# Linear attention with decay and two projections: another order of the instructions behind the opening

## The chip, the cores and the metric

The kernel runs on one core of a Trainium2 chip. The metric is the time of the program on the device in microseconds (us); it is taken as the median of several runs.

## The reference

q, k and v are 4 x 8 x 768 x 64 (batch, heads, positions, head width). Attention goes through blocks of 64 positions with a state of 64 x 64 for each batch and head, and what it gives is the input x (3072 tokens x 512) of two projections with a nonlinear step between them:

```python
for b in range(S // 64):
    intra = einsum('bhic,bhjc->bhij', qb, kb) * Dmask        # lam ** (i - j), i >= j
    intra = einsum('bhij,bhjd->bhid', intra, vb)
    inter = einsum('bhid,bhde->bhie', qb * lam_pow, kv_state)
    out[:, :, sl] = intra + inter
    kv_state = lam_block * kv_state + einsum('bhsd,bhse->bhde', kb * rev_pow, vb)
x = out.transpose(0, 2, 1, 3).reshape(3072, 512)
h = x @ w_in                                                  # 512 x 2048
g = h + sin(alpha * h) ** 2 / (alpha + 1e-9)
y = g @ w_out                                                 # 2048 x 512
```

## The kernel before

The attention is cut into 24 steps, t = 0 to 23, of 128 positions of one batch each. The projections go over 6 chunks, c = 0 to 5, of 512 tokens, four steps each. The program is first recorded as a list of operations, each with a name, an engine, what it reads and writes, and then ordered; the names are those of the lists below:

- "load k9.0e" and the like are transfers by SyncE (SP) of a part of q, k or v (lines 856 and 865); loads number n serves steps 2n and 2n + 1. The tiles k32, q32 and v32 are rings.
- ks, qs and vs with a step's number bring keys, queries and values to bf16 (line 1020 for keys and queries, with a factor; line 1044, a cast, for values). They run on VectorE (DVE), ScalarE (ACT) or GpSimd (POOL). qk2 and v2 are rings too.
- DT is a transposing transfer on SP that turns scaled keys and queries into the layout that TensorE (PE) wants (line 1054).
- S, Z, I and O are PE's scores (line 1096), state (1121, 1147) and outputs (1168) of a step; mask is DVE's product of the scores with the decay (1103, 1109), Zf, Zs the state's copies (1196, 1202, 1208), x the copy of the output to xT (1188).
- A c.m is the first product for one block of 128 of the 2048 columns: four matmuls into one PSUM bank (line 1234). sin c.m (ACT, line 1246), sq c.m (the square, ACT line 1255 or DVE and POOL line 1256) and g c.m follow. g (DVE, line 1260) adds the square, scaled, to the bank's h, and with that gives the bank back. For some columns of chunks 0 and 1 the tokens are taken in halves, h0 and h1.
- B c.s.m4 is a quarter of the second product for 128 tokens: four matmuls (line 1313). After the fourth, o copies the bank (line 1330) and st stores it. The last 128 tokens are done in three pieces of 256, 128 and 128 columns, B5.3.0 to B5.3.2 (lines 1281 to 1292).

There are six PSUM banks in M_ps for A, B and the attention's outputs. Which operation stands where on an engine is a written list, `ORDER`, with one list for each engine; the planner takes an engine's next operation from the head of its list only, and its cost table decides no more than which bank an operation gets. `ON` names the engine of an operation where it can run on several. `GATE` holds transfers back: the operation named on the left also waits for the one on the right.

```python
for a, b in TUNE["GATE"].items():
    named[a].deps.add(named[b])
```

Every engine works through its own list in order, and waits at an operation until what it depends on is done; so one that waits holds up all behind it on its engine.

Of the kernel before, what the change touches and what calls it, by code (L numbers as in the profile page):

```python
# [28 lines left out]
    GATE={'quad q1': 'E_i0',  # L29
          'quad v2': 'ks2',  # L30
          'quad k3': 'R_f',
          'quad k4': 'cT3.0',
          'quad q4': 'cT0.0',
          'quad v4': 'g0.1h0',
          'quad k5': 'g0.8',
# [3 lines left out]
          'quad q7': 'mask3',
          'quad v7': 'sq0.11',  # L40
          'load k4.0e': 'B0.3.3',
          'load v4.0': 'qs10',
          'load v4.0e': 'qs10',
          'load k5.0': 'B0.3.3',
          'load k5.0e': 'sin1.1h0',
          'load v5.0': 'sq1.8',
          'load q5.1': 'A1.0h0',
          'load v6.0': 'ks16',
          'load v6.0e': 'A2.9',
          'load k6.1e': 'g2.0',  # L50
          'load q6.1': 'S10',
          'load q7.0': 'Zs8',
          'load k7.1e': 'O11',
          'DT13': 'sin2.13',
          'load k8.0': 'o7',
          'load v8.0': 'sin2.11',
          'load k8.1': 'g2.4',
          'load k8.1e': 'A2.6',
          'DT15': 'Zs10',
# [1 line left out]
          'load v9.1': 'Z16f',
          'load k10.0': 'B2.2.1',
          'load k10.1': 'sin2.15',
          'load v10.1': 'qs21',
          'load v10.1e': 'A3.9',
          'DT18': 'ks19',
# [16 lines left out]
    ON={'sq2.11': 'DVE',  # L83
        'sq0.14': 'POOL',
        'sq3.0': 'DVE',
        'sq1.0h1': 'ACT',
        'sq2.4': 'ACT',
        'sq4.1': 'ACT',
# [1 line left out]
        'sq3.5': 'ACT',  # L90
        'sq3.14': 'ACT',
        'sq4.4': 'DVE',
        'sq5.14': 'ACT',
        'sq5.15': 'ACT',
        'qs1': 'POOL',
        'sq3.7': 'DVE',
        'sq3.15': 'DVE',
        'sq5.3': 'ACT',
        'vs8': 'POOL',
        'Zs8': 'POOL',  # L100
        'Zs10': 'POOL',
        'sq1.12': 'ACT',
        'sq2.0': 'ACT',
# [1 line left out]
        'sq2.14': 'ACT',
        'sq3.11': 'ACT',
        'sq4.6': 'DVE',
        'sq5.1': 'DVE',
        'qs0': 'POOL',
        'Z1f': 'ACT',  # L110
        'sq0.2h1': 'ACT',
        'sq0.4': 'ACT',
        'sq1.4h0': 'DVE',
        'qs15': 'DVE',
        'Zs14': 'DVE',
        'sq3.12': 'ACT',
        'sq3.13': 'ACT',
        'vs21': 'POOL',
        'cT0.1': 'ACT',
        'qs3': 'POOL',  # L120
        'cT3.0': 'ACT',
        'sq0.15': 'ACT',
        'vs4': 'DVE',
        'ks5': 'DVE',
        'Z6f': 'ACT',
        'qs7': 'POOL',
        'vs7': 'POOL',
# [1 line left out]
        'Z7f': 'ACT',
        'vs11': 'DVE',  # L130
        'Zs17': 'DVE',
        'sq3.8': 'ACT',
        'x19': 'DVE',
        'Zs21': 'DVE',
        'sq4.15': 'DVE',
        'ks1': 'POOL',
        'ks0': 'DVE',
        'Zs1': 'ACT',
        'Zs2': 'DVE',
        'Zs3': 'DVE',  # L140
        'sq0.0h0': 'POOL',
        'sq0.7': 'ACT',
        'sq0.9': 'DVE',
        'qs4': 'POOL',
        'qs5': 'POOL',
        'vs5': 'POOL',
        'cT6.1': 'ACT',
        'qs14': 'DVE',
        'x14': 'DVE',
        'sq3.4': 'DVE',  # L150
        'sq3.10': 'ACT',
        'ks20': 'DVE',
        'sq4.0': 'DVE',
        'ks21': 'DVE',
        'vs22': 'DVE',
        'sq4.8': 'ACT',
        'sq4.12': 'ACT',
        'sq5.4': 'ACT',
        'sq5.5': 'ACT',
        'o20': 'DVE',  # L160
        'o21': 'DVE',
        'Z2f': 'ACT',
        'Zi3': 'DVE',
        'sq0.0h1': 'DVE',
        'sq0.5': 'DVE',
        'sq0.8': 'POOL',
        'sq0.13': 'ACT',
        'cT4.1': 'ACT',
        'Zs4': 'POOL',
        'qs6': 'POOL',  # L170
        'Zs6': 'POOL',
        'o2': 'DVE',
        'ks8': 'DVE',
        'ks9': 'DVE',
        'vs9': 'DVE',
        'x8': 'DVE',
        'sq1.6': 'DVE',
        'sq1.7': 'DVE',
        'Zs9': 'DVE',
        'ks11': 'DVE',  # L180
        'sq1.10': 'POOL',
        'sq1.11': 'ACT',
        'qs12': 'DVE',
        'sq1.14': 'ACT',
        'sq1.15': 'POOL',
        'Zs11': 'DVE',
        'ks13': 'DVE',
        'sq2.10': 'ACT',
        'vs15': 'DVE',
        'sq2.12': 'ACT',  # L190
        'ks17': 'DVE',
        'sq3.1': 'ACT',
        'vs17': 'DVE',
        'o8': 'DVE',
        'sq3.3': 'ACT',
        'sq3.6': 'ACT',
        'ks19': 'DVE',
        'sq3.9': 'ACT',
        'qs19': 'DVE',
        'vs19': 'DVE',  # L200
        'o10': 'DVE',
        'qs21': 'DVE',
        'x20': 'DVE',
        'ks22': 'DVE',
        'ks23': 'DVE',
        'sq4.9': 'DVE',
        'qs23': 'DVE',
        'sq4.10': 'DVE',
        'o14': 'DVE',
        'sq4.11': 'DVE',  # L210
        'sq4.14': 'ACT',
        'x23': 'DVE',
        'sq5.2': 'DVE',
        'sq5.6': 'ACT',
        'sq5.7': 'POOL',
        'o18': 'DVE',
        'sq5.11': 'POOL',
        'sq5.13': 'ACT'},
# [1248 lines left out]
```

## Time and profile before

| | us |
|---|---|
| median of three runs | 214.68 (214.08 to 215.11) |
| profiled execution | 216.0 |
| its span | 214.1 |
| PE busy | 204.3 |
| DVE, ACT, POOL busy | 140.9, 127.0, 69.3 |

The profile is of one execution. Its span is what the trace covers; the time beside it is the device's. The granted clock of PE was 1.00 throughout. Rows of the timeline give the start, the time, the engine, the line, the operation and its tiles, and in brackets how long the engine had been idle before and what ended that.

### The profile page before, as it was taken

How to read it: one execution, taken by the hardware profiler on the slowest of the kernel's cores; microseconds unless marked ns; L12 is line 12 of the kernel's file. 1: busy time of each engine (PE TensorE's matmuls, PEld its weight loads, DVE VectorE, ACT ScalarE, POOL GpSimd, SP SyncE). 2: the span in 40 equal slices, each digit the busy share in tenths (PEclk: the TensorE clock that was granted, in tenths of full speed). 3: DMA queues.
4: the chain of work that ended last, by engine and by line, in shares of the span. 5: the costliest groups of instructions: out<-in, count | busy, mean ns of one | idle time of the engine just before them, and what ended most of it. 6: DMA issues, size and time to landing. Idle time of an engine off the chain costs nothing.

```text
span 214.1 us, 5329 instructions
## 1 busy us (share of the span) xinstructions
PE 204.3 (95%) x2216; PEld 112.8 (53%) x2216; DVE 140.9 (66%) x245; ACT 127.0 (59%) x233; POOL 69.3 (32%) x88
## 2 busy tenths in 40 slices
PE   7898999999799999999999998899999999999995
PEld 7657654657555455444455543344555444454454
DVE  2497795767789862685667866958879744355511
ACT  3662989936787337877445598624665716657411
POOL 4397129810176205654700130400411101116100
PEclk9999999999999999999999999999999999999999
DMA  6999999987998899777899889989521201050015
GB/s 178 276 256 212 216 219 275 230 184 185 200 163 179 177 191 233 142 216 164 177 161 236 179 174 186 157 196 154 123 52 49 90 11 49 2 194 3 0 63 182
DMA packets 86985, 33.90 MB, mean 158 GB/s; under 512 B 68786, under 2 KB 83506, under 8 KB 86962
## 3 DMA queue, kind: packets, MB, share of 16 engines
q1 hardware_dynamic: 79616, 22.88, 54.0%
q0 software_dynamic: 2688, 4.19, 11.1%
q10 hardware_dynamic: 4658, 6.50, 8.6%
q8 instruction: 17, 0.28, 0.5%
q14 instruction: 6, 0.05, 0.1%
HBM read 27.27 MB, written 6.29 MB: 157 GB/s over the span
## 4 chain that ended last, share of the span: by engine, by line
PE 64%; DMA 19%; DVE 6%; ACT 4%; POOL 3%; issue 2%; SPq 1%; ACTq 0%; DVEq 0%; POOLq 0%
PE M_ps L1313 30%; PE M_ps L1234 25%; DMA q<-in_q_dram 8%; DMA k<-in_k_dram 5%; DMA w<-in_moe_w_out_dram 4%; DVE gT L1260 3%; DMA alpha_sb<-in_moe_alpha_dram 3%; PE M_ps L1147 2%; POOL qk L1020 2%; PE M_ps L1281 2%; ACT t L1246 2%; PE A_ps L1096 2%; PE M_ps L1168 1%; DVE qkT L1071 1%; ACT u L1255 1%
## 5 line engine op out<-in xcount | busy, mean ns | idle before, releaser
L1234 PE MATMUL M_ps<-xT,w 128*128 128x512 bf16 (+1 forms) x424 | 88.6, 359 | 2.4 <-DVE gT L1260 2.3
L1260 DVE SCALAR_TENSOR_TENSOR gT<-u,r_sb,M_ps 128x512 bf16<-128x512 bf16 (+1 forms) x106 | 69.8, 692 | 30.1 <-POOL u L1256 15.3
L1313 PE MATMUL M_ps<-w,gT 128*128 128x512 bf16 x368 | 87.8, 380 | 1.2 <-DVE gT L1260 0.8
L1246 ACT ACTIVATE t<-M_ps,alpha_sb 128x512 bf16<-128x512 f32 (+1 forms) x106 | 65.2, 646 | 32.2 <-PE M_ps L1234 28.5
L1234 PEld LDWEIGHTS M_ps<-xT,w 128*128 128x128 bf16 x424 | 46.6, 114 | 39.0 <-DVE gT L1260 4.1
L1256 POOL TENSOR_TENSOR u<-t 128x512 bf16<-128x512 bf16 x27 | 27.9, 1041 | 86.0 <-ACT t L1246 81.9
L1313 PEld LDWEIGHTS M_ps<-w,gT 128*128 128x128 bf16 x368 | 34.1, 98 | 40.5 <-DVE gT L1260 1.8
L1255 ACT ACTIVATE u<-t 128x512 bf16<-128x512 bf16 x46 | 28.4, 628 | 0.9 <-ACT t L1246 0.2
L1020 POOL TENSOR_TENSOR qk<-q,L 128x512 bf16<-128x512 f32 x14 | 14.5, 1045 | 23.3 <-DVE qk L1020 14.8
L1188 ACT CAST xT<-M_ps 128x512 bf16<-128x512 f32 x14 | 8.1, 587 | 21.2 <-PE M_ps L1121 17.5
L1109 DVE TENSOR_TENSOR S_m<-A_ps,maskl 128x768 bf16<-128x768 f32 x16 | 15.2, 951 | 3.1 <-PE M_ps L1147 1.7
L1256 DVE TENSOR_TENSOR u<-t 128x512 bf16<-128x512 bf16 x23 | 10.1, 443 | 6.0 <-ACT t L1246 5.8
L1020 POOL TENSOR_TENSOR qk<-k,L 128x512 bf16<-128x512 f32 x9 | 9.4, 1045 | 10.6 <-DMA k<-in_k_dram 10.5
L1330 ACT COPY osb<-M_ps 128x512 f32<-128x512 f32 x13 | 7.6, 585 | 8.4 <-PE M_ps L1313 8.3
L826 PE MATMUL M_ps<-zeros 128*128 128x128 bf16 (+1 forms) x62 | 8.4, 317 | 1.2 <-DVE zeros L903 1.2
L1330 DVE COPY osb<-M_ps 128x512 f32<-128x512 f32 x7 | 4.7, 685 | 7.3 <-PE M_ps L1313 7.3
L1121 PE MATMUL M_ps<-v,qk 64*64 64x64 bf16 x320 | 8.3, 193 | 0.9 <-DVE S_m L1103 0.7
L1168 PE MATMUL M_ps<-S_m,v 64*64 64x128 bf16 (+1 forms) x384 | 9.0, 208 | 0.0
L1103 DVE TENSOR_TENSOR S_m<-A_ps,maskq 128x1024 bf16<-128x1024 f32 x6 | 7.3, 1218 | 2.1 <-PE A_ps L1096 2.1
L1020 DVE TENSOR_TENSOR qk<-k,L 128x512 bf16<-128x512 f32 x11 | 7.4, 683 | 1.8 <-DMA k<-in_k_dram 1.8
L1202 DVE TENSOR_TENSOR Zf<-M_ps,Zf 128x256 f32<-128x256 f32 x12 | 5.0, 420 | 5.4 <-ACT xT L1188 5.3
L1096 PE MATMUL A_ps<-qkT 64*64 64x128 bf16 (+1 forms) x352 | 8.2, 210 | 0.2 <-DVE qkT L1071 0.2
(72 smaller groups left out, 135.0 us busy)
## 6 DMA issues: line engine op xcount, KB each, us to landing
q<-in_q_dram SPq DMA_DIRECT2D x24, 256.0 KB, 5.4
out_dram<-osb ACTq DMA_DIRECT2D x23, 256.0 KB, 2.3
v<-in_v_dram SPq DMA_DIRECT2D x32, 128.0 KB, 4.3
k<-in_k_dram SPq DMA_DIRECT2D x32, 128.0 KB, 4.6
v<-in_v_dram SPq DMA_DIRECT2D x8, 256.0 KB, 5.4
w<-in_moe_w_in_dram POOLq DMA_DIRECT2D x4, 512.0 KB, 10.1
w<-in_moe_w_out_dram POOLq DMA_DIRECT2D x4, 512.0 KB, 10.1
k<-in_k_dram SPq DMA_DIRECT2D x7, 256.0 KB, 5.3
```

Source lines behind the costliest of these rows:

```text
L826: last = e.matmul(m_ps[i][:, 0:c], zeros[:, 0:128], zeros[:, 0:c])
L1020: rec(en, lambda e, ll=ll, xs=xs: e.tensor_tensor(o[:, :, xs], i[:, :, xs], ll, ALU.mult), *(((0.65, 0.58) if en == "DVE" else (1.04, 1.0) ...
L1096: last = e.matmul(Av[ps, h, a, ek, 0:128 - q0], T[rows, 1, a, ek, ps], T[rows, 0, a, i, q0:128])
L1109: rec("DVE", lambda e: e.tensor_tensor(S_m[jm][:, :, :].rearrange("p (a b) c -> p a (b c)", a=4)[:, :, 0:192], S_ps().rearrange("p (a b) c ...
L1168: res = e.matmul(bank(i)[64 * a:64 * a + 64, h, qs], vv[ps, h, a, ek, :], Sv[ps, h, a, ek, 0:qs.stop - qs.start], start=(op0 and i == 0 an ...
L1234: last = e.matmul(m_ps[vb.i][:, N * i:N * i + N], w1[:, kc, cols(mm)], xT[x][:, kc, ts], start=(kc == 0 and i == 0), stop=(kc == NKC - 1), ...
L1246: rec("ACT", lambda e, i=i, mm=mm: e.activation(t16[tt][:, N * i:N * i + N], m_ps[vb.i][:, N * i:N * i + N], ACTF.Sin, scale=alpha_sb[:, m ...
L1255: return e.activation(u16[tt][:, :], t16[tt][:, :], ACTF.Square)
L1256: return e.tensor_tensor(u16[tt][:, :], t16[tt][:, :], t16[tt][:, :], ALU.mult)
L1260: rec("DVE", lambda e, i=i, mm=mm: e.scalar_tensor_tensor(out=gT[g][:, mm, ts], in0=u16[tt][:, N * i:N * i + N], scalar=r_sb[:, mm:mm + 1] ...
L1313: last = e.matmul(m_ps[vb.i], gT[g][:, m, 128 * s4:128 * (s4 + 1)], w2[:, m, :], start=(m == 0 or (split and m == 8)), stop=(m == NM - 1 o ...
L1330: rec(en, lambda e: cp(e)(osb[o][:, :], m_ps[vb.i]), *((0.585, 0.48) if en == "ACT" else (0.65, 0.58)), reads=[vb.key], writes=[f"o.{o}"], ...
```

## The change

Three tables change: `GATE`, `ON` and `ORDER`. The rest of the program is the same text, 13 lines further down, so that line 1020 before is line 1033 after, and so on. The operations are the same; 104 of the entries in `ON` differ. The lists are the same up to A1.0h0 on PE, sq1.4h0 on DVE, sin1.3h0 on ACT, vs7 on POOL and "load q5.1" on SP, some 53 us into the program. In `GATE` 15 entries are kept, 9 name another event, 20 are new and 17 are gone.

```diff
     GATE={...
+          'load k11.0': 'B2.3.0',
+          'load k9.0e': 'O13',
...
+          'DT19': 'sin3.9',
...
-          'load k9.0e': 'sq3.7',
...
-          'DT19': 'g3.12',
-          'load k11.0': 'A3.13',
...
     ORDER={...
             'DVE': [...
-                   'o3', 'Z5f', 'Z4f', 'o2', 'mask7', 'x7', 'sq1.4h0', 'g1.4h0', 'sq1.2h0', 'ks8', 'g1.5h0',
...
-                   'g3.8', 'o10', 'sq3.7', 'g3.5', 'g3.6', 'g3.7', 'qs19', 'ks21', 'ks20', 'vs19', 'g3.11',
-                   'g3.9', 'Zs11', 'ks19', 'g3.12', 'mask17', 'g3.10', 'sq3.15', 'g3.14', 'g3.15', 'vs17',
...
+                   'o3', 'Z5f', 'Z4f', 'o2', 'mask7', 'x7', 'sq1.4h0', 'x6', 'Z7f', 'g1.3h0', 'maskl2',
+                   'g1.2h0', 'g1.5h0', 'g1.1h0', 'g1.4h0', 'g1.0h0', 'sq1.7', 'g1.7', 'g1.6', 'o1', 'g1.3h1',
+                   'g1.2h1', 'g1.4h1', 'ks8', 'g1.1h1', 'g1.0h1', 'sq1.9', 'g1.5h1', 'g1.9', 'g1.8', 'g1.11',
...
+                   'Zs12', 'Zs13', 'mask15', 'Z14f', 'mask16', 'qs20', 'Z15f', 'sq3.3', 'g3.3', 'g3.0', 'ks19',
+                   'sq3.2', 'g3.1', 'sq3.8', 'g3.8', 'sq3.6', 'Zs15', 'g3.6', 'g3.5', 'g3.2', 'g3.10', 'sq3.4',
```

The first place is DVE just behind the common part, where it works on chunk 1. qk2_2<-k32 is ks8, the short gT sums are g1.3h0, g1.2h0 and so on. Before:

```order
L1188 CAST xT_1<-M_ps 128x2x2x128
L1256 TENSOR_TENSOR u16_3<-t16_3 128x512
L1260 SCALAR_TENSOR_TENSOR gT_1<-u16_3,r_sb,M_ps 128x256
L1256 TENSOR_TENSOR u16_2<-t16_2 128x512
L1020 TENSOR_TENSOR qk2_2<-k32,L 128x2x4x64
L1260 SCALAR_TENSOR_TENSOR gT_1<-u16_3,r_sb,M_ps 128x256
L1260 SCALAR_TENSOR_TENSOR gT_1<-u16_2,r_sb,M_ps 128x256 x2
```

After:

```order
L1201 CAST xT_1<-M_ps 128x2x2x128
L1269 TENSOR_TENSOR u16_3<-t16_3 128x512
L1201 CAST xT_1<-M_ps 128x2x2x128
L1209 COPY Zf_3<-M_ps 128x128
L1273 SCALAR_TENSOR_TENSOR gT_1<-u16_2,r_sb,M_ps 128x256
L971 COPY maskl<-maskl 64x192
L1273 SCALAR_TENSOR_TENSOR gT_1<-u16_2,r_sb,M_ps 128x256
L1273 SCALAR_TENSOR_TENSOR gT_1<-u16_3,r_sb,M_ps 128x256
L1273 SCALAR_TENSOR_TENSOR gT_1<-u16_1,r_sb,M_ps 128x256
L1273 SCALAR_TENSOR_TENSOR gT_1<-u16_3,r_sb,M_ps 128x256
L1273 SCALAR_TENSOR_TENSOR gT_1<-u16_1,r_sb,M_ps 128x256
```

x6 and Z7f (line 1201 and 1209) have come in from other engines, and ks8 has gone further back: in the whole list it stands seven rows below the last one shown.

The second place is DVE in chunk 3. In the list of before, qk2_1<-q32 is qs19, the next two rows are ks21 and ks20, v2_1<-v32 is vs19, the sum behind it g3.11, and qk2_1<-k32 further down is ks19:

```order
L1020 TENSOR_TENSOR qk2_1<-q32,L 128x2x4x64
L1020 TENSOR_TENSOR qk2_3<-k32,L 128x2x4x64
L1020 TENSOR_TENSOR qk2_2<-k32,L 128x2x4x64
L1044 CAST v2_1<-v32 128x512
L1260 SCALAR_TENSOR_TENSOR gT_1<-u16_4,r_sb,M_ps 128x512
L1260 SCALAR_TENSOR_TENSOR gT_1<-u16_2,r_sb,M_ps 128x512
L1208 CAST Zq_1<-Zf_1 128x256
L1020 TENSOR_TENSOR qk2_1<-k32,L 128x2x4x64
L1260 SCALAR_TENSOR_TENSOR gT_1<-u16_0,r_sb,M_ps 128x512
```

After, ks20 and ks21 are on POOL and vs19 is on ACT. qk2_1<-k32 is ks19, which now stands behind the sums g3.3 and g3.0:

```order
L1215 TENSOR_TENSOR Zf_3<-M_ps,Zf_3 128x256
L1269 TENSOR_TENSOR u16_1<-t16_1 128x512
L1273 SCALAR_TENSOR_TENSOR gT_1<-u16_1,r_sb,M_ps 128x512
L1273 SCALAR_TENSOR_TENSOR gT_1<-u16_3,r_sb,M_ps 128x512
L1033 TENSOR_TENSOR qk2_1<-k32,L 128x2x4x64
L1269 TENSOR_TENSOR u16_0<-t16_0 128x512
L1273 SCALAR_TENSOR_TENSOR gT_1<-u16_4,r_sb,M_ps 128x512
L1269 TENSOR_TENSOR u16_1<-t16_1 128x512
L1273 SCALAR_TENSOR_TENSOR gT_1<-u16_1,r_sb,M_ps 128x512
```

ks19 has come forward past sums of chunk 3 that stood ahead of it, and squares have come in between the sums.

The third place is SP from DT18 on before and from DT19 on after; qkT_2, qkT_3, qkT_0 and qkT_1 are the transposes DT18 (DT22), DT19 (DT23), DT20 and DT21. Before:

```order
L1054 DMA_TRANSPOSE qkT_2<-qk2_0 128x8x128
L1054 DMA_TRANSPOSE qkT_3<-qk2_1 128x8x128
L1054 DMA_TRANSPOSE qkT_0<-qk2_2 128x8x128
L865 DMA v32<-in_v_dram 64x8x64
L865 DMA k32<-in_k_dram 64x8x64 x3
L865 DMA v32<-in_v_dram 64x8x64
L1054 DMA_TRANSPOSE qkT_1<-qk2_3 128x8x128
L1054 DMA_TRANSPOSE qkT_2<-qk2_4 128x8x128
L865 DMA v32<-in_v_dram 64x8x64
L1054 DMA_TRANSPOSE qkT_3<-qk2_5 128x8x128
```

After, qkT_3<-qk2_1 is DT19; the three loads behind it are v10.1e, v10.1 and v9.0e, and those between DT20 (qkT_0) and DT21 (qkT_1) are v11.0, v11.1 and v10.0e:

```order
L1067 DMA_TRANSPOSE qkT_3<-qk2_1 128x8x128
L878 DMA v32<-in_v_dram 64x8x64 x3
L1067 DMA_TRANSPOSE qkT_2<-qk2_0 128x8x128
L878 DMA k32<-in_k_dram 64x8x64 x2
L878 DMA v32<-in_v_dram 64x8x64
L1067 DMA_TRANSPOSE qkT_0<-qk2_2 128x8x128
L878 DMA v32<-in_v_dram 64x8x64 x3
L1067 DMA_TRANSPOSE qkT_1<-qk2_3 128x8x128
L1067 DMA_TRANSPOSE qkT_2<-qk2_4 128x8x128
L1067 DMA_TRANSPOSE qkT_3<-qk2_5 128x8x128
```

Before, all the values of steps up to 21 and one of the last were loaded ahead of DT18; after, value loads stand between the transposes, and DT18 comes after DT19.

On PE ten blocks of the first product of chunk 4 now follow one another, and then ten of the second product; before, at most five of the first stood together there. At the end, the 256-column piece of the last 128 tokens (B5.3.0) is now PE's last, and the 128-column pieces go ahead of it.

More of the change, by code (lines that the diff above doesn't have):

```diff
@@ L28 @@
     SPAIR=(1, 3),
-    GATE={'quad q1': 'E_i0',
-          'quad v2': 'ks2',
[L31 to L35, printed above, removed]
+    GATE={'load v4.1': 'o2',
+          'load k11.0': 'B2.3.0',
+          'load k4.0e': 'B0.3.3',
+          'load k9.0e': 'O13',
+          'load k10.1e': 'sq2.15',
+          'quad q7': 'mask3',
+          'load v8.0e': 'sin3.3',
+          'st23.1': 'o21',
+          'load v4.0': 'qs10',
+          'load k6.1e': 'sq1.0h1',
+          'load k5.0e': 'B0.3.3',
+          'load v7.0e': 'A2.0',
+          'load v11.0': 'vs18',
+          'quad k5': 'g0.8',
+          'load k7.1e': 'S11',
+          'load v11.0e': 'sq3.7',
+          'load k11.1': 'sq3.11',
+          'load q10.0': 'B1.0.2',
+          'load v6.1': 'sq2.2',
+          'quad v6': 'Z5',
+          'DT11': 'sq1.13',
+          'load q7.1': 'sq2.8',
+          'quad k4': 'cT3.0',
+          'load q9.0': 'mask10',
+          'load q6.0': 'sq1.2h1',
+          'DT18': 'A3.9',
+          'DT17': 'o10',
+          'quad k3': 'R_f',
+          'load v11.1': 'vs17',
+          'quad q1': 'E_i0',
+          'DT13': 'sq2.6',
+          'quad q4': 'cT0.0',
+          'load k10.1': 'vs14',
+          'DT22': 'B3.0.3',
+          'quad v4': 'g0.1h0',
+          'load q8.0': 'B1.1.3',
+          'quad v7': 'sq0.11',
+          'quad v2': 'ks2',
@@ L36 @@
           'quad q6': 'Z0',
-          'quad v6': 'Z5',
+          'load k5.0': 'B0.3.3',
           'quad k7': 'B0.1.0',
[L39 to L59, printed above, removed]
-          'load k9.0e': 'sq3.7',
[L61 to L66, printed above, removed]
@@ L67 @@
-          'DT19': 'g3.12',
-          'load k11.0': 'A3.13',
-          'DT23': 'A4.4'},
+          'DT19': 'sin3.9',
+          'DT9': 'sin1.13',
+          'load q11.1': 'qs21'},
     SPLIT=(1, 1, 0, 1),
@@ L82 @@
          dict(k='POOL', q='DVE', v='ACT', c=('ACT', 'DVE'), z='ACT', x='ACT', f='DVE', w='ACT')),
-    ON={'sq2.11': 'DVE',
-        'sq0.14': 'POOL',
[L85 to L88, printed above, removed]
-        'sq2.7': 'ACT',
[L90 to L103, printed above, removed]
-        'sq2.9': 'ACT',
[L105 to L127, printed above, removed]
-        'x7': 'DVE',
[L129 to L218, printed above, removed]
@@ new lines @@
+    ON={'Z1f': 'ACT',
+        'sq3.6': 'DVE',
+        'sq0.0h1': 'DVE',
+        'sq0.13': 'ACT',
+        'o20': 'DVE',
+        'sq0.4': 'ACT',
+        'qs4': 'POOL',
+        'o6': 'DVE',
+        'vs8': 'POOL',
+        'sq3.7': 'ACT',
+        'sq1.0h0': 'POOL',
+        'vs13': 'POOL',
+        'qs20': 'DVE',
+        'Zs0': 'ACT',
+        'sq1.4h1': 'ACT',
+        'sq3.13': 'DVE',
+        'sq4.5': 'ACT',
+        'sq5.0': 'DVE',
+        'vs18': 'POOL',
+        'sq4.4': 'ACT',
+        'sq1.7': 'DVE',
+        'sq4.3': 'DVE',
+        'Zi3': 'DVE',
+        'sq1.0h1': 'ACT',
+        'Zs6': 'POOL',
+        'ks8': 'DVE',
+        'sq5.15': 'ACT',
+        'Zs3': 'DVE',
+        'sq1.4h0': 'DVE',
+        'x23': 'DVE',
+        'sq2.8': 'ACT',
+        'sq3.8': 'DVE',
+        'sq5.4': 'DVE',
+        'o8': 'DVE',
+        'cT0.1': 'ACT',
+        'sq2.4': 'ACT',
+        'Z6f': 'ACT',
+        'o19': 'DVE',
+        'ks22': 'DVE',
+        'vs7': 'POOL',
+        'ks17': 'DVE',
+        'sq2.15': 'DVE',
+        'sq4.2': 'DVE',
+        'sq4.1': 'ACT',
+        'sq0.2h1': 'ACT',
+        'vs11': 'POOL',
+        'sq3.14': 'ACT',
+        'qs5': 'POOL',
+        'sq4.8': 'ACT',
+        'sq4.0': 'DVE',
+        'sq3.10': 'ACT',
+        'Zs1': 'ACT',
+        'sq5.14': 'DVE',
+        'Zs9': 'DVE',
+        'sq5.13': 'ACT',
+        'o17': 'DVE',
+        'cT4.1': 'ACT',
+        'o22': 'DVE',
+        'sq2.5': 'ACT',
+        'Z2f': 'ACT',
+        'sq0.15': 'ACT',
+        'sq1.13': 'DVE',
+        'sq2.13': 'ACT',
+        'sq1.12': 'ACT',
+        'vs20': 'DVE',
+        'sq0.14': 'POOL',
+        'Zs10': 'DVE',
+        'sq1.9': 'DVE',
+        'sq2.3': 'ACT',
+        'sq3.15': 'ACT',
+        'x21': 'DVE',
+        'qs6': 'POOL',
+        'Zs8': 'POOL',
+        'qs0': 'POOL',
+        'x10': 'DVE',
+        'sq5.5': 'DVE',
+        'sq0.9': 'DVE',
+        'sq1.14': 'POOL',
+        'Zs15': 'DVE',
+        'sq5.2': 'ACT',
+        'Zs13': 'DVE',
+        'qs1': 'POOL',
+        'sq5.7': 'ACT',
+        'Zs21': 'POOL',
+        'sq5.12': 'DVE',
+        'sq5.6': 'DVE',
+        'sq1.6': 'ACT',
+        'cT6.1': 'ACT',
+        'sq2.0': 'DVE',
+        'sq4.13': 'DVE',
+        'sq1.2h0': 'POOL',
+        'sq5.1': 'ACT',
+        'ks1': 'POOL',
+        'sq0.8': 'POOL',
+        'sq4.7': 'DVE',
+        'Zs11': 'POOL',
+        'sq4.10': 'DVE',
+        'Zs12': 'DVE',
+        'qs7': 'POOL',
+        'sq0.7': 'ACT',
+        'sq2.10': 'ACT',
+        'sq1.8': 'ACT',
+        'sq2.2': 'DVE',
+        'Zs5': 'POOL',
+        'sq3.9': 'DVE',
+        'vs10': 'DVE',
+        'sq5.10': 'DVE',
+        'x6': 'DVE',
+        'cT3.0': 'ACT',
+        'o21': 'DVE',
+        'vs15': 'DVE',
+        'vs23': 'DVE',
+        'sq3.1': 'ACT',
+        'vs22': 'DVE',
+        'ks5': 'DVE',
+        'qs21': 'DVE',
+        'sq2.12': 'DVE',
+        'ks0': 'DVE',
+        'sq1.15': 'POOL',
+        'vs5': 'POOL',
+        'vs4': 'DVE',
+        'Zs14': 'DVE',
+        'sq2.7': 'ACT',
+        'o7': 'DVE',
+        'o14': 'DVE',
+        'sq4.15': 'DVE',
+        'ks11': 'DVE',
+        'vs12': 'POOL',
+        'sq3.4': 'DVE',
+        'sq3.2': 'DVE',
+        'sq3.3': 'DVE',
+        'o13': 'DVE',
+        'sq0.0h0': 'POOL',
+        'x22': 'DVE',
+        'ks19': 'DVE',
+        'sq0.5': 'DVE',
+        'qs3': 'POOL',
+        'vs21': 'DVE',
+        'sq2.9': 'ACT',
+        'o2': 'DVE',
+        'Zs2': 'DVE',
+        'ks12': 'DVE',
+        'sq4.11': 'ACT',
+        'x7': 'DVE',
+        'qs15': 'DVE'},
```

147 rows, old and new, of the table ORDER are left out of this document.

## The prediction

> **What bounds the kernel now.** I read the busy table of the page first, then the windows of five microseconds, then the timeline of PE and of VectorE (DVE) in the windows that are not full, and last the groups by form.
>
> ```profile
> span 214.1 us, 5329 instructions
> ...
> PE 204.3 (95%) x2216; PEld 112.8 (53%) x2216; DVE 140.9 (66%) x245; ACT 127.0 (59%) x233; POOL 69.3 (32%) x88
> ```
>
> PE is the bound: it is busy 204.3 of 214.1 us, and no other engine comes near. The change alters no matmul, so it can gain only what PE idles. The windows show where that is, from 50 us on, where the order begins to differ (columns: PE, PEld, DVE, ACT, POOL busy with counts, granted clock, DMA share, GB/s). These seven are all the windows below 5.00 before the last:
>
> ```profile
> 55.00:60.00 5.00, 3.72 (x25) 2.45 (x24) 4.49 (x11) 3.51 (x8) 1.29 (x2) 1.00 0.95 204
> 75.00:80.00 5.00, 4.80 (x150) 2.74 (x153) 3.41 (x7) 1.71 (x4) 0.41 (x1) 1.00 0.98 187
> 100.00:105.00 5.00, 4.95 (x38) 2.06 (x35) 2.60 (x4) 3.41 (x8) 5.00 (x6) 1.00 0.82 169
> 105.00:110.00 5.00, 4.74 (x127) 2.61 (x128) 3.90 (x7) 2.44 (x5) 0.45 (x2) 1.00 1.33 188
> 130.00:135.00 5.00, 4.02 (x20) 1.81 (x19) 3.24 (x6) 3.80 (x7) 1.04 (x1) 1.00 1.31 189
> 135.00:140.00 5.00, 4.52 (x22) 1.96 (x21) 4.38 (x7) 3.90 (x7) 1.60 (x3) 1.00 0.88 164
> 170.00:175.00 5.00, 4.89 (x68) 2.34 (x66) 3.64 (x6) 2.25 (x4) 0.00 (x0) 1.00 0.15 56
> ```
>
> The idle time is 1.28 + 0.20 + 0.05 + 0.26 + 0.98 + 0.48 + 0.11 = 3.36 us. Two places hold 2.74 of it. At the first, DVE stands for a load:
>
> ```profile
> 55.51 0.69 DVE L1020 TENSOR_TENSOR qk<-k,L 128x512 bf16<-128x512 f32 x1 [1.57 <-DMA k<-in_k_dram]
> 56.12 1.26 DVE L1260 SCALAR_TENSOR_TENSOR gT<-u,r_sb,M_ps 128x256 bf16<-128x256 bf16 x3
> ...
> 56.65 1.93 PE L1234 MATMUL M_ps<-xT,w 128*128 128x256 bf16 x12 [1.04 <-DVE gT L1260]
> 58.81 1.93 PE L1234 MATMUL M_ps<-xT,w 128*128 128x256 bf16 x12 [0.24 <-DVE gT L1260]
> ```
>
> A key scale stood 1.57 us for its load. Behind it in DVE's list were the sums (L1260) that give PSUM banks back, and PE had no bank to write to. The second place is the same thing twice over:
>
> ```profile
> 132.94 0.43 DVE L1044 CAST v<-v 128x512 bf16<-128x512 f32 x1 [1.76 <-issue]
> 133.28 1.40 DVE L1260 SCALAR_TENSOR_TENSOR gT<-u,r_sb,M_ps 128x512 bf16<-128x512 bf16 x2
> ...
> 132.06 1.03 PE L1313 MATMUL M_ps<-w,gT 128*128 128x512 bf16 x4
> 134.07 1.92 PE L1234 MATMUL M_ps<-xT,w 128*128 128x512 bf16 x8 [0.98 <-DVE gT L1260]
> 136.47 2.33 PE L1313 MATMUL M_ps<-w,gT 128*128 128x512 bf16 x10 [0.48 <-DVE gT L1260]
> ...
> 81.23 7.77 PE M_ps L1234 x36
> ```
>
> The value cast vs19 stood 1.76 us ("issue" is the page's word for a wait it cannot name; the operand is a loaded tile), the sum g3.11 stood behind it, and PE stood at 134.07 and 136.47. The last row, from the chain of waits, is PE's undisturbed pace: 36 matmuls in 7.77 us, 0.863 for a block of four. By it the stall costs more than its idle figure: from 132.06 to 134.07 are 2.01 us for one block, a loss of 1.15 where the row says 0.98, and from 134.07 to 136.47 are 2.40 for two, a loss of 0.67 where it says 0.48. I add 0.18 to each of the seven stalls: 1.26.
>
> **The change part by part.**
>
> *Stalls that go.* I walked PE's new list with 0.863 per block of four and this for an attention group (state, scores and output of one step):
>
> ```profile
> 151.09 0.25 PE L1147 MATMUL M_ps<-qkT,Zq 64*64 64x128 bf16 x4
> ...
> 151.89 3.64 PE L1234 MATMUL M_ps<-xT,w 128*128 128x512 bf16 x16
> ```
>
> so 0.80 us each, and set beside it when each engine can have done what a block needs, by these groups:
>
> ```profile
> L1260 DVE SCALAR_TENSOR_TENSOR gT<-u,r_sb,M_ps 128x512 bf16<-128x512 bf16 x86 | 61.7, 743 | 27.8 <-ACT u L1255 14.3 <-POOL u L1256 13.2
> L1246 ACT ACTIVATE t<-M_ps,alpha_sb 128x512 bf16<-128x512 f32 x86 | 56.7, 685 | 26.9 <-PE M_ps L1234 23.4 <-DVE u L1256 2.4 <-POOL u L1256 0.9
> L1255 ACT ACTIVATE u<-t 128x512 bf16<-128x512 bf16 x46 | 28.4, 628 | 0.9 <-ACT t L1246 0.2
> L1256 POOL TENSOR_TENSOR u<-t 128x512 bf16<-128x512 bf16 x27 | 27.9, 1041 | 86.0 <-ACT t L1246 81.9 <-DVE gT L1260 3.3 <-DVE qk L1020 0.6
> L1256 DVE TENSOR_TENSOR u<-t 128x512 bf16<-128x512 bf16 x23 | 10.1, 443 | 6.0 <-ACT t L1246 5.8
> L1020 POOL TENSOR_TENSOR qk<-k,L 128x512 bf16<-128x512 f32 x9 | 9.4, 1045 | 10.6 <-DMA k<-in_k_dram 10.5
> L1044 POOL CAST v<-v 128x512 bf16<-128x512 f32 x4 | 2.8, 692 | 0.0
> L1109 DVE TENSOR_TENSOR S_m<-A_ps,maskl 128x768 bf16<-128x768 f32 x16 | 15.2, 951 | 3.1 <-PE M_ps L1147 1.7 <-PE A_ps L1096 1.4
> ```
>
> At the first place the scale ks8 moves behind nine of the short sums, two long ones and some copies; I put it at 60 us, while its load, up to which SP's list is all but unchanged, lands by 55.51. Its wait is gone and nothing bank-giving stands behind a load there. At the second place vs19 leaves DVE for ACT, ks20 and ks21 leave for POOL, and only ks19 is left on DVE, behind g3.0. The three remaining waits (79 us, 105 us, 171 us) are of the same kind, a bank or a mask that came 0.1 to 0.3 late, and in the walk the blocks there find theirs ready. I found no place where PE has to wait by the order itself; the smallest margins are 0.3 to 0.5 us. So all of 3.36 + 1.26 = 4.6 us goes, as an estimate from these rows.
>
> *Work that changes engine.* By the lists squares go from 46/23/27 on ACT, DVE and POOL to 39/35/22, key and query scales from 17/23 on DVE and POOL to 10/30, four output copies from ACT to DVE, three value casts from ACT to POOL. DVE gets 12 x 0.44 - 7 x 0.69 + 4 x 0.69 = about 3 us more, POOL 7 x 1.045 + 3 x 0.69 - 5 x 1.041 = 4.2 more, ACT some 8 less. I cost this at nothing: PE's 95% is the cover, with DVE at 66%. The one stretch where the cover is thin is the fifth chunk, where PE now runs ten first-product blocks in a row, 16 of them with only two attention groups among them: 16 x 0.863 + 1.6 = 15.4 us. DVE needs 16 sums at 0.70 (1.40 for two, above), 7 squares, 2 masks and about 3 us of copies: 11.2 + 3.1 + 1.9 + 3 = 19.2. It falls 3.8 us behind. Behind the run stand ten second-product blocks, 8.6 us, that need none of these sums, so the lag is made up there.
>
> *A rule against it.* One pair of rows shows DVE and POOL in each other's way:
>
> ```profile
> 138.32 0.61 POOL L1044 CAST v<-v 128x512 bf16<-128x512 f32 x1
> 138.40 0.81 DVE L1256 TENSOR_TENSOR u<-t 128x512 bf16<-128x512 bf16 x1 [0.46 <-ACT t L1246]
> ```
>
> The square took 0.81 us where the mean is 0.443. That is 0.37 more beside a POOL instruction. Squares and scales on DVE number 40 before and 45 after, POOL is busy 32% before and about 34% after, so meetings go from 13 to 15; two more, at 0.37, are 0.7 us of DVE, hidden. The Trainium skill, "SBUF — State Buffer", section "SBUF: two separate sides", says that the port pair shared by VectorE and GpSimd is locked by one of them for a whole instruction, by a vector operation with two SBUF inputs among others, and the other blocks fully. The pair of rows agrees. By that rule alone, each new meeting could cost up to what the POOL instruction lasts, and the change would be worse off for every square that it moves to DVE; the sum would then be that of the second rival below.
>
> *Loads and transposes.* Of the table of events that hold back loads, transposes and one store, 9 entries name another event, 20 are new and 17 are gone, and from the load of q5.1 on all of SP's list is another one. These rows price them (us from issue to landing, then the time SP needs to issue one):
>
> ```profile
> k<-in_k_dram SPq DMA_DIRECT2D x32, 128.0 KB, 4.6
> v<-in_v_dram SPq DMA_DIRECT2D x32, 128.0 KB, 4.3
> qkT<-qk SPq DMA_TRANSPOSE x16, 3.8
> ...
> 126.83 1.47 SPq L865 DMA_DIRECT2D k<-in_k_dram x2
> ...
> 135.84 4.75 SPq L1054 DMA_TRANSPOSE qkT<-qk x3
> ```
>
> Two places are thin. The first: the last load that ks19 needs is the seventh on SP behind one that waits for block B2.3.0, done at 107 in the walk; with 0.74 each it is issued at 112 and lands near 117, and DVE comes to ks19 at 117.3. Behind ks19 stand the sums of chunk 3. The second: SP must, in this order, issue the transpose DT19 (after sin3.9), three loads, DT20 and three loads and DT21, on which PE's scores S21 rest, and DT20 waits for ks20, which stands on POOL behind vs18, whose value load is the third. That chain is 0.7 + 1.6 + 3 x 0.74 + 4.3 + 0.7 + 1.05 + 1.6 + 3 x 0.74 + 3.8 = 18.2 us, and up to 19.3 if the issues run slower; PE has 19 blocks and four groups until then, 16.4 + 3.3 = 19.7. I charge each place 0.4 us, between nothing and the 1.82 that the place at 133 lost: the first margin is 0.3, the second 0.4 to 1.5, and a load's landing spreads by more than that.
>
> *The tail.* The last two narrow blocks change places, so the end is a copy of 256 columns and its store:
>
> ```profile
> 210.70 0.37 ACT L1289 COPY osl<-M_ps 128x256 f32<-128x256 f32 x1 [1.20 <-PE M_ps L1281]
> ...
> 211.60 0.29 DVE L1289 COPY osl<-M_ps 128x128 f32<-128x128 f32 x1 [2.17 <-PE M_ps L1281]
> ...
> out_dram<-osl ACTq DMA_DIRECT2D x1, 128.0 KB, 1.8
> out_dram<-osl SPq DMA_DIRECT2D x1, 64.0 KB, 1.6
> ```
>
> 0.08 + 0.2 = about 0.2 us more.
>
> **The sum.** The profiled execution took 216.0 us: 216.0 - 4.6 + 0.2 + 0.8 = 212.4. That execution was 1.3 above the median of the runs, 214.68; carried onto it, the change of -3.6 gives 211.1 us. If the extra 1.3 lay in these very stalls, the gain is 1.3 smaller and the time 212.4.
>
> **The rivals.** *Late loads take the place of the stalls.* The stalls of before were loads that came late to an engine with bank-giving work behind them, and the new order has two such places with margins below the spread of a load. For it speaks that the same two waits cost 1.82 us at 133; against it, that fewer such instructions stand on DVE. One place lost in full gives 214.68 - 4.4 + 1.8 = 212.1, two give 213.9, and a third 215.7; I take 213.9.
>
> *DVE and POOL lock each other out: slower.* Place: 100 to 150 us, where POOL's new scales and casts lie beside most of the 12 new squares on DVE. Price: a square that meets a 1.045 us scale waits half of it, 0.52; with all 12 on the path 6.3 us, and 214.68 - 4.4 + 6.3 = 216.6. It makes the kernel measurably slower from 4.4 + 1.07 = 5.5 us of loss, 11 squares. For it speaks the square of 0.81; against it, that the mean of all 23 is 0.443, so few were caught, and that DVE gives up seven scales.
>
> That the lists are not followed I can leave out: the order of the instructions is that of the lists.
>
> **How the numbers follow.** A measurement of this kernel can tell 0.5%, 1.07 us: 213.6 to 215.75 is no change. The forecast has 0.66, with a range of its own of 209.6 (no thin place shows, 210.3, less the 0.6 that the runs spread) to 212.6 (the 1.3 above). Late loads have 0.22, half of it below 213.6: 0.11 faster, 0.10 no change, 0.01 slower. The lock has 0.10, all slower. Both together have 0.02, slower. So faster 0.77, same 0.10, slower 0.13. The range goes from 209.6 to 214.6 and leaves out the lock, both together and the upper end of the late loads.
>
> **What would show it.** Right: PE's windows from 50 to 205 us full; no DVE row that stands over a microsecond for a load ahead of sums; PE's busy time within 0.5 us of before and the span near 210.5. The first rival would show as a wait of ks19, or of the scores at the start of the fifth chunk for qkT. The second would show as a mean DVE square well above 0.443 with DVE nearly full from 100 to 150. I am wrong if PE idles 2 us or more in new places, or if the idle time goes and the span stays.

## The result and the profile after

The changed kernel took 213.11 us (median of 16 runs, 211.70 to 216.41), the kernel before 214.74 (16 runs, 214.08 to 216.70). The ratio is 0.9918, with a 95% interval of 0.9894 to 0.9943. Ratios leave out the runs that took over 1.5% longer than the fastest of their kernel, and the profiled execution of before, 216.0 us, is on record as one of those. So the changed kernel is faster, by 1.6 us where 3.6 were forecast: the time lies in the range, the gain is less than half.

The profiled execution took 212.83 us, span 211.0. Here are its busy table, the windows that answer to those shown of before, and two that are new (columns as there):

```profile
PE 202.7 (96%) x2216; PEld 112.1 (53%) x2216; DVE 147.0 (70%) x256; ACT 118.8 (56%) x217; POOL 73.2 (35%) x93
```

```profile
55.00:60.00 5.00, 5.00 (x31) 2.93 (x29) 3.79 (x9) 3.96 (x9) 3.08 (x3) 1.00 1.11 212
80.00:85.00 5.00, 4.20 (x91) 2.44 (x91) 2.60 (x6) 1.46 (x3) 0.00 (x0) 1.00 0.85 205
115.00:120.00 5.00, 5.00 (x25) 2.52 (x24) 2.33 (x5) 3.25 (x5) 1.04 (x1) 1.00 0.84 193
130.00:135.00 5.00, 5.00 (x25) 2.42 (x24) 4.30 (x6) 4.07 (x7) 3.21 (x4) 1.00 0.61 127
135.00:140.00 5.00, 5.00 (x76) 2.52 (x75) 3.32 (x7) 2.68 (x5) 2.53 (x3) 1.00 0.84 171
170.00:175.00 5.00, 5.00 (x83) 2.41 (x82) 2.84 (x4) 0.59 (x1) 0.00 (x0) 1.00 0.02 3
```

All the stalls of before are gone, as the walk had it. One new loss of 0.80 us stands at 80 us. PE stops there in the middle of one attention group's matmuls, and the releaser is the page's "issue", a wait it cannot name.

```profile
80.20 0.26 PE L1181 MATMUL M_ps<-S_m,v 64*64 64x128 bf16 x8
81.26 0.27 PE L1181 MATMUL M_ps<-S_m,v 64*64 64x128 bf16 x6 [0.81 <-issue]
```

Between these two profiles the difference is what was forecast: 216.0 - 212.83 = 3.2 us, where 3.6 were summed. Between the medians it is half of that. The profiled execution of before was 1.3 us above its median, that of after 0.3 below. Theory A: the stalls of before follow loads that land at different times in each execution, and the first profile had them long. Theory B: they are always that long, and the new order loses the gain again in ways that its one profile doesn't show.

### The profile page after: what moved, and what is told of

It is laid out like the page before. It is cut to its first block, busy times and chain, and to the rows that moved or that the text cites. A ratio compares the mean times of both kernels' runs of the same rounds, so it can differ in the third digit from the quotient of the medians.

```text
span 211.0 us, 5339 instructions
## 1 busy us (share of the span) xinstructions
PE 202.7 (96%) x2216; PEld 112.1 (53%) x2216; DVE 147.0 (70%) x256; ACT 118.8 (56%) x217; POOL 73.2 (35%) x93
## 4 chain that ended last, share of the span: by engine, by line
PE 78%; DMA 13%; POOL 5%; issue 1%; SPq 1%; ACT 1%; DVE 0%; POOLq 0%; ACTq 0%
PE M_ps L1247 36%; PE M_ps L1326 34%; DMA w<-in_moe_w_in_dram 6%; DMA w<-in_moe_w_out_dram 4%; DMA v<-in_v_dram 3%; POOL qk L1033 2%; PE M_ps L1160 2%; PE A_ps L1109 2%; PE M_ps L1294 2%; PE M_ps L1181 1%; PE M_ps L1134 1%; POOL w L901 1%; SPq L889 1%; POOL v L1053 0%; POOL u L1269 0%
## 5 line engine op out<-in xcount | busy, mean ns | idle before, releaser
L1259 ACT ACTIVATE t<-M_ps,alpha_sb 128x512 bf16<-128x512 f32 (+1 forms) x106 | 65.9, 645 | 36.0 <-PE M_ps L1247 30.0
L1269 POOL TENSOR_TENSOR u<-t 128x512 bf16<-128x512 bf16 x22 | 22.8, 1041 | 78.8 <-ACT t L1259 57.2
L1269 DVE TENSOR_TENSOR u<-t 128x512 bf16<-128x512 bf16 x35 | 16.1, 459 | 14.5 <-ACT t L1259 14.2
L1268 ACT ACTIVATE u<-t 128x512 bf16<-128x512 bf16 x39 | 24.2, 626 | 0.7
L1033 POOL TENSOR_TENSOR qk<-q,L 128x512 bf16<-128x512 f32 x17 | 17.6, 1044 | 8.4 <-DMA q<-in_q_dram 3.3
L1033 POOL TENSOR_TENSOR qk<-k,L 128x512 bf16<-128x512 f32 x13 | 13.5, 1045 | 11.5 <-DMA k<-in_k_dram 11.4
L1343 ACT COPY osb<-M_ps 128x512 f32<-128x512 f32 x9 | 5.3, 585 | 12.9 <-PE M_ps L1326 12.9
L1343 DVE COPY osb<-M_ps 128x512 f32<-128x512 f32 x11 | 7.5, 686 | 3.7 <-PE M_ps L1326 3.6
L1109 PEld LDWEIGHTS A_ps<-qkT 64*64 64x64 bf16 x352 | 5.6, 107 | 4.3 <-DVE qkT L1084 1.2
L1181 PEld LDWEIGHTS M_ps<-S_m,v 64*64 64x64 bf16 x384 | 6.8, 107 | 0.9 <-issue 0.9
```

Source lines behind the costliest of these rows:

```text
L1033: rec(en, lambda e, ll=ll, xs=xs: e.tensor_tensor(o[:, :, xs], i[:, :, xs], ll, ALU.mult), *(((0.65, 0.58) if en == "DVE" else (1.04, 1.0) ...
L1109: last = e.matmul(Av[ps, h, a, ek, 0:128 - q0], T[rows, 1, a, ek, ps], T[rows, 0, a, i, q0:128])
L1181: res = e.matmul(bank(i)[64 * a:64 * a + 64, h, qs], vv[ps, h, a, ek, :], Sv[ps, h, a, ek, 0:qs.stop - qs.start], start=(op0 and i == 0 an ...
L1259: rec("ACT", lambda e, i=i, mm=mm: e.activation(t16[tt][:, N * i:N * i + N], m_ps[vb.i][:, N * i:N * i + N], ACTF.Sin, scale=alpha_sb[:, m ...
L1268: return e.activation(u16[tt][:, :], t16[tt][:, :], ACTF.Square)
L1269: return e.tensor_tensor(u16[tt][:, :], t16[tt][:, :], t16[tt][:, :], ALU.mult)
```

## The experiments

### The same two kernels again

> The kernel before, unchanged, for a second profile of it. Theory A (the profiled execution of before, 1.3 us above the median, had stalls that most executions do not have): PE idles some 2.1 us or less from 50 to 205 us where the first profile had 3.36, most of what is missing at 133 us, and the profiled execution takes about 214.7. Theory B (the stalls of before are there in every execution, and the new order loses them again elsewhere): the windows 55 to 60 and 130 to 140 show the same 1.28 and 1.46 us as in the first profile.

> The kernel before, a third profile. Theory A (loads land at different times from execution to execution, and the stalls of before follow them): from the start of A1.0h0 to PE's last matmul some 156.3 to 158 us, with the first two profiles at 158.75 and 156.48, and the two large places again the ones that differ. Theory B (the first profile is the rule): 158.5 or more.

> The kernel before, a fourth profile; the same two expectations, 156.3 to 158 us by theory A, 158.5 or more by theory B. A mean of the four above 158 would leave theory A without its number.

> The changed kernel, unchanged, for a second profile of it. Theory A: again no wait of PE for a bank or a load of more than 0.3 us behind 50 us; the only loss is a pause inside an attention group as at 80 us, in this place or another; time 1.6 us below before. Theory B: a wait of PE behind 50 us that the first profile does not have, of 0.5 us or more, for a load or for a bank whose sum stands behind a load.

> The changed kernel, a third profile. Theory A: from A1.0h0 to PE's last matmul 154.4 to 155.5 us, with what differs between executions in the opening ahead of A1.0h0. If late loads do stop PE in it now and then (rival 1 of the prediction), one place of 0.5 us or more behind a load.

> The changed kernel, a fourth profile; the same as of the third: 154.4 to 155.5 us by theory A, and a place of 0.5 us or more behind a load if rival 1 happens now and then.

Each row is the window from the start of A1.0h0, where the orders part, to PE's last matmul: its limits, its length, PE busy and the rest. First before, four executions (the first is the one that the prediction read; the last two of each kernel ran on another chip than the second):

```profile
52.81:211.56 158.75, 155.38 (x1528) 80.38 (x1528) 104.74 (x174) 92.75 (x164) 43.74 (x48) 1.00 0.65 138
```

```profile
52.62:209.10 156.48, 154.92 (x1528) 80.45 (x1528) 105.03 (x174) 92.84 (x164) 43.80 (x48) 1.00 0.66 139
```

```profile
53.92:210.97 157.05, 152.46 (x1507) 80.39 (x1528) 104.77 (x174) 92.80 (x164) 43.75 (x48) 1.00 0.65 139
```

```profile
52.62:210.01 157.39, 152.45 (x1507) 80.35 (x1528) 105.25 (x174) 92.85 (x164) 43.80 (x48) 1.00 0.67 139
```

Then the changed kernel, four executions:

```profile
52.84:208.23 155.39, 154.58 (x1528) 80.53 (x1528) 110.81 (x186) 84.23 (x147) 48.06 (x53) 1.00 0.67 142
```

```profile
54.69:209.15 154.46, 154.46 (x1528) 80.42 (x1528) 110.99 (x186) 84.16 (x147) 48.10 (x53) 1.00 0.67 142
```

```profile
52.88:207.77 154.89, 152.18 (x1504) 80.39 (x1528) 110.61 (x186) 84.14 (x147) 48.54 (x53) 1.00 0.68 142
```

```profile
52.80:208.88 156.08, 152.31 (x1504) 80.47 (x1528) 110.91 (x186) 84.21 (x147) 47.96 (x53) 1.00 0.67 141
```

The reader is to look at the lengths. (In the last two of each kernel some matmul records are missing, 1507 or 1504 of 1528, so their PE busy is too low; the lengths stand.) The second row of the changed kernel has no idle time at all: 154.46 us is the floor of this stretch. Before stands 4.3, 2.0, 2.6 and 2.9 above it, and the profile that was read is the largest. The changed kernel stands 0.9, 0.0, 0.4 and 1.6 above it. The means differ by 157.42 - 155.21 = 2.2, without the profile that was read by 1.8. This is theory A, with a little of B: the changed kernel does lose something now and then. The pause at 80 us stands in two of four. In the fourth, whose 156.08 us lie above the 155.5 that theory A allowed, PE also waited 0.43 us for the state's sum. The rows of POOL, DVE and PE lead back to a late load:

```profile
105.93 1.04 POOL L1033 TENSOR_TENSOR qk<-k,L 128x512 bf16<-128x512 f32 x1 [2.03 <-DMA k<-in_k_dram]
106.93 1.04 POOL L1033 TENSOR_TENSOR qk<-q,L 128x512 bf16<-128x512 f32 x1
107.12 1.41 DVE L1033 TENSOR_TENSOR qk<-k,L 128x512 bf16<-128x512 f32 x1
109.78 1.90 PE L1326 MATMUL M_ps<-w,gT 128*128 128x512 bf16 x8 [0.43 <-DVE Zf L1215]
```

A key scale on POOL waited 2.03 us, so the query scale behind it ran beside a key scale of DVE. That one took 1.41 us, where it took 0.68 in the first and third profile and 0.87 in the second, and the mask and the state's sum behind it came late.

The two large places in the other profiles of before, first the second profile with PE's waits behind each place, then DVE alone in the third and the fourth:

```profile
54.65 0.69 DVE L1020 TENSOR_TENSOR qk<-k,L 128x512 bf16<-128x512 f32 x1 [0.90 <-DMA k<-in_k_dram]
55.78 1.93 PE L1234 MATMUL M_ps<-xT,w 128*128 128x256 bf16 x12 [0.36 <-DVE gT L1260]
...
130.85 0.43 DVE L1044 CAST v<-v 128x512 bf16<-128x512 f32 x1 [1.37 <-issue]
131.99 1.92 PE L1234 MATMUL M_ps<-xT,w 128*128 128x512 bf16 x8 [0.61 <-DVE gT L1260]
```

```profile
55.85 0.69 DVE L1020 TENSOR_TENSOR qk<-k,L 128x512 bf16<-128x512 f32 x1 [0.80 <-DMA k<-in_k_dram]
...
132.55 0.43 DVE L1044 CAST v<-v 128x512 bf16<-128x512 f32 x1 [1.93 <-issue]
```

```profile
55.10 0.69 DVE L1020 TENSOR_TENSOR qk<-k,L 128x512 bf16<-128x512 f32 x1 [1.35 <-DMA k<-in_k_dram]
...
131.74 0.43 DVE L1044 CAST v<-v 128x512 bf16<-128x512 f32 x1 [1.86 <-issue]
```

ks8 waits 0.80 to 1.57 us for the same load in the same program, vs19 1.37 to 1.93. The places are always the same; their size is not. PE idles 1.56 us in the second profile's stretch, 3.37 in the first's. Theory A had this below 2.1, but most of the difference at 133 us: 0.68 of it lies at the first place, 0.61 at the second. The page calls the wait of vs19 "issue". It ends with a load all the same. vs19 needs four loads, the last of them on SP is v9.0e, and in the profile that was read this is its row:

```profile
128.34 0.64 SPq L865 DMA_DIRECT2D v<-in_v_dram  x1
```

It landed 4.5 us after its issue, at 132.8, and vs19 began at 132.94. In the other three profiles, too, vs19 began within 0.1 us of that landing.

In the times, before against itself gave 1.0001 (0.9974 to 1.0028), and the changed kernel in the same comparison 0.9959 (0.9927 to 0.9991): a smaller gain than in the first, 0.9 us, where theory A had 1.6, with intervals that overlap. Part of that goes with the granted clock of PE. Eight of the twelve runs of the changed kernel had a mean clock of 0.992, of before's only a third. Among the other runs, at 0.998 or more, the means are 212.50 and 213.75 us, among those at 0.992 they are 213.51 and 214.75: a gain of about 1.25 in each.

### Only the two large stalls taken out of before

```diff
-  'sq1.2h0', 'ks8', 'g1.5h0', 'g1.3h0', 'g1.2h0', 'ks9',
+  'sq1.2h0', 'g1.5h0', 'g1.3h0', 'g1.2h0', 'ks8', 'ks9',
...
-  'ks21', 'ks20', 'vs19', 'g3.11', 'g3.9', 'Zs11', 'ks19', 'g3.12', 'mask17',
+  'ks21', 'ks20', 'g3.11', 'g3.9', 'g3.12', 'vs19', 'Zs11', 'ks19', 'mask17',
```

> The kernel before with only the two large stalls taken out: on DVE the scale ks8 behind the sums g1.5h0, g1.3h0 and g1.2h0, and vs19 and ks19 behind g3.11, g3.9 and g3.12. Everything else, the banks too, is as before. Theory A: the two places are worth 1.6 us of first place in every execution but little of second place: about 2.1 us faster than before at most, 0.5 at least. Theory B: both are worth what the first profile shows, 1.6 and 1.8: 3.4 us faster, and faster than the changed kernel. A rival C: PE is then held by the next thing, the scores of step 18 or 19 whose keys are scaled later, and the gain is under 0.5 us.

Measured: 212.50 us (12 runs), ratio 0.9925 (0.9894 to 0.9956), so 1.6 us faster. Two edits of one engine's list, with the banks kept as they were, do what the whole new order does. Theory B's 3.4 us lies outside the interval, which ends at 2.3; rival C's 0.5 lies outside it too. The stretch:

```profile
53.29:208.22 154.93, 154.52 (x1528) 80.48 (x1528) 105.20 (x174) 92.72 (x164) 43.76 (x48) 1.00 0.65 141
```

It is 0.5 above the floor, as short as the changed kernel's.

> As the kernel with both places, but only vs19 and ks19 moved behind g3.11, g3.9 and g3.12. Theory A: 0 to 0.5 us faster than before. Theory B: 1.8 us faster.

The second line of the diff alone gave 0.9984 (0.9959 to 1.0009), 0.3 us: as theory A had it, but not for its reason. The wait at 133 us is gone, and another stands behind it. ACT, then DVE, then PE:

```profile
135.21 0.62 ACT L1044 CAST v<-v 128x512 bf16<-128x512 f32 x1 [1.50 <-DMA v<-in_v_dram]
135.73 1.84 ACT L1246 ACTIVATE t<-M_ps,alpha_sb 128x512 bf16<-128x512 f32 x3
```

```profile
137.67 0.68 DVE L1256 TENSOR_TENSOR u<-t 128x512 bf16<-128x512 bf16 x1 [1.41 <-ACT t L1246]
```

```profile
139.44 1.90 PE L1313 MATMUL M_ps<-w,gT 128*128 128x512 bf16 x8 [0.91 <-DVE gT L1260]
```

A value cast on ACT waits 1.50 us for its load; three sines stand behind it, a square of DVE waits for one of them, and PE for a bank. In the first profile of before the same cast waited as long, but PE, late at 133 itself, did not wait a second time for it:

```profile
135.93 0.62 ACT L1044 CAST v<-v 128x512 bf16<-128x512 f32 x1 [1.63 <-DMA v<-in_v_dram]
```

In the profile with both places moved the same cast waited 0.57, and PE did not wait there:

```profile
132.83 0.62 ACT L1044 CAST v<-v 128x512 bf16<-128x512 f32 x1 [0.57 <-DMA v<-in_v_dram]
```

### One load made late, in each kernel

```diff
-  'load k4.1', 'load q4.1', 'load q4.0', 'load q5.0',
+  'load q4.1', 'load q4.0', 'load q5.0', 'load k4.1',
```

In before, three entries of `GATE` come with it; each holds an operation of POOL for one of DVE (qs8 for ks9, sq1.4h1 for maskl2, qs11 for sq1.8). The changed kernel with the late load has none of them.

> The kernel before with the load k4.1, for which the scale ks8 stands at 55 us, issued three places later on SP, behind three query loads of 256 KB. It should land some 3.5 us later (estimate: the three take 2.6 us longer to move than nothing does, and 0.7 each to issue). Theory A (the stalls of before follow the landing of loads, one for one, and that landing differs between executions): the wait at the first place grows by what the load is later, and the kernel is 2.5 to 3.5 us slower than before. Rival D (the stall is set by something else, the banks or the squares behind it): under 1 us slower.

> The same load as late in the changed kernel. Theory A: there ks8 runs 9.3 us behind A1.0h0 and the load lands at about 5.5, so nothing waits: the time is that of the changed kernel, within 0.4 us. Rival E (the new order only has its loads earlier by luck): 1 us slower or more.

Before became slower, 218.72 us, ratio 1.0204 (1.0139 to 1.0270); the changed kernel with the same late load stayed at 213.06, ratio 0.9950 (0.9915 to 0.9984) against before. Before with the late load on DVE and PE, then the changed kernel with it on DVE:

```profile
59.33 0.69 DVE L1020 TENSOR_TENSOR qk<-k,L 128x512 bf16<-128x512 f32 x1 [4.70 <-DMA k<-in_k_dram]
...
53.50 2.80 PE L1234 MATMUL M_ps<-xT,w 128*128 128x256 bf16 x20
60.47 1.93 PE L1234 MATMUL M_ps<-xT,w 128*128 128x256 bf16 x12 [1.79 <-DVE gT L1260]
```

```profile
62.80 1.33 DVE L1033 TENSOR_TENSOR qk<-k,L 128x512 bf16<-128x512 f32 x1
```

```profile
53.50:213.61 160.11, 157.46 (x1540) 81.59 (x1540) 104.79 (x174) 92.77 (x164) 43.74 (x48) 1.00 0.64 136
```

ks8 waited 4.70 us where it waited 0.80 to 1.57. Between the two rows of PE no matmul of the two products runs for 60.47 - 53.50 - 2.80 = 4.17 us, where it was 0.27 to 1.04 in the four profiles of before: at this place PE loses 3.5 us more than in their mean, as much as ks8 waits longer. (Eleven matmuls of zeros that the planner put there fill a part, so the row says 1.79.) The stretch, whose row is the last, was only 2.7 us longer than the mean of before; one reason is the second place, where PE waited 0.72 us against 1.46 in the profile that was read. The ratio says 4.4 us, 3.0 to 5.8, from three runs; why it is more than the profile's 2.7, and whether the three entries of `GATE` have a part in it, stays open. In the profile PE has no wait of 0.15 us or more between 63 and 136 us. In the changed kernel ks8 didn't wait at all. That rules out rival D, and rival E for this load. But the profile of the changed kernel with the late load also has the first rival of the prediction, once, at another key scale of DVE. It waited 0.47 us, and then took 1.28 where it took 0.68 in the first profile of the changed kernel; scales of POOL, themselves late for a load, ran beside it. Sums stand behind it:

```profile
89.58 1.28 DVE L1033 TENSOR_TENSOR qk<-k,L 128x512 bf16<-128x512 f32 x1 [0.47 <-DMA k<-in_k_dram]
```

```profile
91.91 1.27 PE L1247 MATMUL M_ps<-xT,w 128*128 128x512 bf16 x5 [0.57 <-DVE gT L1273]
```

### The tail

```diff
-  'B5.1.3', 'B5.3.1', 'B5.0.3', 'B5.3.2', 'B5.3.0'],
+  'B5.1.3', 'B5.0.3', 'B5.3.2', 'B5.3.0', 'B5.3.1'],
...
-  'o21', 'o23.1', 'o22', 'o20'],
+  'o21', 'o22', 'o20', 'o23.1'],
```

> The changed kernel with the end of before: the three narrow blocks of the last 128 tokens come as 128, 256 and 128 columns again, behind B5.0.3. If the tail costs what the prediction said, the time from the last matmul to the end falls from 2.74 to 2.77 back to about 2.5 us, and the kernel is 0.2 us faster than the changed one. If the end is set by the stores that queue ahead, nothing changes. Either way no wait of PE from 53 to 205 us.

From the last matmul to the end of the span were 211.0 - 208.23 = 2.77 us in the changed kernel; here they are 210.7 - 208.14 = 2.56. So the tail costs what was forecast, 0.2. The time is 212.49 us, ratio 0.9931 (0.9901 to 0.9961): faster than before, and not to be told from the changed kernel (0.9918 and 0.9959) or from the one with two moves (0.9925).

## Why the prediction was wrong

The direction and the mechanism were right: PE idled because sums that give banks back stood behind an operation that waited for a load, the new order takes them out from behind it, and PE's stretch is full where it was not.

**The term that was mis-sized is the first, 4.6 us for the stalls.** It was read from one execution, 1.3 us above the median, and the difference was carried onto the median as it stood. For that execution it was nearly right: its stretch stood 4.3 us above the floor. In three others it was 2.0, 2.6 and 2.9, in the mean 2.5. The prediction saw the 1.3 and named this case ("if the extra 1.3 lay in these very stalls"), yet kept it for an edge, 212.4. The runs show that it was the case: A1.0h0 began at 52.81 us in that execution, not late beside 52.62 to 53.92 in the others, so the excess lay in the stretch with the stalls. With 2.5 for the stalls and the 0.7 that the changed kernel's stretch loses, both measured, the sum is 214.7 - 2.5 + 0.2 + 0.7 = 213.1.

That 213.11 lies in the range is luck in part: it is above the forecast's own 209.6 to 212.6, in the part that was added for late loads taking the place of the stalls, and they took it only in small pieces.

**Its signs.** PE's windows from 55 to 205 us are full but for the one at 80. Two signs of being right failed: ks19 stood more than a microsecond for a load ahead of sums, which cost PE nothing, and PE's busy time fell by 1.6 us where less than 0.5 was named, half of it ahead of A1.0h0, where the orders are the same. The window from 50 to 55 us, 4.78 before, was left out of the seven; it is 4.78 after as well.

**The thin places: the size right by luck, the places wrong.** 0.8 us was charged to ks19 and to the scores S21. The last load of ks19 came 1.41 us after DVE was free for it:

```profile
118.03 0.75 DVE L1273 SCALAR_TENSOR_TENSOR gT<-u,r_sb,M_ps 128x512 bf16<-128x512 bf16 x1 [0.78 <-POOL u L1269]
120.19 0.69 DVE L1033 TENSOR_TENSOR qk<-k,L 128x512 bf16<-128x512 f32 x1 [1.41 <-DMA k<-in_k_dram]
```

DVE was busy for 2.33 of the 5.00 us from 115 to 120 (the row above), and PE was full there and in the next windows: it did not need the sums behind ks19 sooner. The scores S21 began without idle time ahead of them:

```profile
148.13 0.37 PE L1109 MATMUL A_ps<-qkT 64*64 64x128 bf16 x16
```

The 0.7 us by which the changed kernel's mean stands above the floor are in the main the pause at 80 us and the wait of 0.43 in the fourth profile; the rest was not taken apart.

**The tail, 0.2:** right. **Work moved between engines, nothing:** right; DVE went from 141 to 147 us, where about 3 more were summed, and its run in the fifth chunk cost PE nothing.

**The lock of DVE and POOL** did not decide. The mean square on DVE was 443, 463, 448 and 468 ns in the four profiles of before, and 459, 434, 447 and 447 in those of the changed kernel, so the 12 squares more did not make it longer. The row of the first profile after:

```profile
L1269 DVE TENSOR_TENSOR u<-t 128x512 bf16<-128x512 bf16 x35 | 16.1, 459 | 14.5 <-ACT t L1259 14.2
```

Single operations are caught, and two that were reached PE: the key scales of 1.41 and 1.28 us above, with 0.43 and 0.57 us of PE behind them. In both a late load had put the POOL scale beside them, so this is the first rival and the second at once, at a small size. A third is in the kernel with the second place moved: the cast vs19 took 1.17 us where it took 0.43, beside a POOL scale of 1.04:

```profile
132.76 1.17 DVE L1044 CAST v<-v 128x512 bf16<-128x512 f32 x1
```

```profile
132.61 1.04 POOL L1020 TENSOR_TENSOR qk<-k,L 128x512 bf16<-128x512 f32 x1 [4.64 <-DMA k<-in_k_dram]
```

The Trainium skill, "SBUF — State Buffer", section "SBUF: two separate sides", says that of a DVE operation with two SBUF inputs or in a two-port mode and a GpSimd one, the one that starts first holds the shared pair of ports for its whole instruction, and the other is blocked. The key scale of 1.41 us, which has two inputs, agrees with it: POOL's scale began first, and DVE's ended 0.56 us after that was done, where it takes 0.68 alone. No run here took the scales off POOL to show it.
